# Attention and gated FFN on one core: v products and copies of the first steps rearranged, masks built later

## The chip, the cores and the metric

The kernel runs on one core of one Trainium2 chip. The metric is the device time of one execution in microseconds. Three executions of the kernel before took 215.73, 215.87 and 215.88 us; the median is 215.87.

## What is computed

The input x has 2048 rows of 448 bf16 values. A layer norm without gain gives xn, and the output is x plus two branches that both read xn:

```python
xn = layernorm(x)                                    # per row, eps 1e-5
q, k, v = split(xn @ wqkv)                           # 16 heads of 28 columns
scores = q k^T * 28**-0.5, kept where 0 <= i - j < 256
A = softmax(scores) v @ wo
B = (gelu(xn @ w_gate) * (xn @ w_up)) @ w_down       # inner width 1792
out = x + A + B
```

Each query looks at itself and the 255 keys before it.

## The kernel before

The rows are taken as 16 tiles of 128, in four blocks (`qb`) of 512 rows. The 448 columns of xn are held transposed in `xnT` as three chunks of 128 and one of 64; the last chunk stands twice, in partitions 0 to 63 and in 64 to 127. So a product over the columns is three matmuls of 128 rows and a "half" of 64 rows. Two halves that use different row groups of TensorE can run side by side. For v, `v_dense(t, pv)` (line 219) issues the three full chunks of row tile t and `v_half` (222) the half, in the upper row group for odd t and the lower for even t; `v_copy` (225) then moves the PSUM bank into `v_sb`. For q and k, the heads stand in four groups `g` of four heads; `proj` issues three full chunks, `qk_halves` the half of q (lower row group) and of k (upper), and `qk_copies` (242) moves q through ScalarE, or another engine if one is passed, and k through VectorE.

Nothing is scheduled by a planner: the program runs in a manual schedule, and each engine executes its instructions in the order in which the Python code emits them. For block 0 the order is written as a list `plan` with one entry for each of nine steps of attention. A step `i` emits, in this order: sometimes the product of probabilities with v for a finished head group (`pv`, tile `ov`); its score matmuls (tile `sc`, line 599) into the only score buffer; one exp on ScalarE over 128 x 2048 (line 603) into `p_sb`; the causal and window masking on GpSimd (POOL) by two or three `affine_select` instructions (line 527); and then whatever `plan[i]` lists. An entry `(u, 3)` advances the generator `u` three times. In block 0, `u` first runs `gen_qk` (259) for the groups 1, 2 and 3, three advances per group (q chunks; k chunks; halves and copies), and then `gen_up` (408), seven advances for each up projection `p` of the FFN (tile `ue`, seven pairs of 64-row matmuls, then two copies into `hT`, line 418). Other entries are functions: `stat(t)` takes the row statistics of tile t on VectorE, `rstd` turns them into a scale on ScalarE, `norm(t)` writes the normalised rows on VectorE (line 169), and `dma_transp(t)` transposes them into `xnT` through a DMA of the SP queue (line 175). The functions `ahead`, `ahead2` and `ahead3` (706 to 737) hold such work for the tiles 4 to 7, the exchanges of half columns (`swap`, SP queue), `fill_pads` on POOL (lines 283 and 285) and the weight loads that follow on the SP queue.

PSUM for all of this comes from four banks, `b0` to `b3`. A list `spare` holds the free ones:

```python
    def take(name, cols=QB, tag=None):
        tag = tag or spare[0]
        spare.remove(tag)
    def give(*tiles):
        for ps in tiles:
            spare.append(held.pop(id(ps))[0])
```

A bank is given back in the program as soon as its copy has been emitted; on the chip the next user waits until the copy is done. So the order in which tiles are given decides which copy a later product waits for. Before the first step the v tiles 0 and 1 have been copied, and the tiles `pvs[2]` (bank b2) and `pvs[3]` (b3) are open: `v_dense(3)` is issued ahead of step 0 (line 702), `v_dense(2)` in step 1. Their halves and copies are passed to `gen_qk` as `others`: tile 3 with group 1, tile 2 with group 2.

The weights of q and k are copied from the loaded `wraw` into padded layouts `wqp` and `wkp` by `pads` (646; the copies are line 651), group by group: group 0 early, group 1 on VectorE, and groups 2 and 3 together on VectorE (line 704). `masks` are 0/1 patterns for the blocks from 1 on. VectorE fills them with ones (line 133), and `make_masks` (109) cuts them with 18 `affine_select` instructions on POOL (line 115), ahead of step 0. They are first used in block 1 (line 517).

After the attention steps of a block, `gated` (422) runs seven gate projections (`gt`, line 401), and after each multiplies into `hT`; it calls `hook(2 * p)` (780) after projection p, which emits softmax sums and scalings and the norms of tiles 8 to 11.

Of the kernel before, what the change touches and what calls it, by code (L numbers as in the profile page):

```python
# [17 lines left out]
P = 128  # L18
# [8 lines left out]
def kernel(  # L27
# [11 lines left out]
    nc = tc.nc  # L39
# [133 lines left out]
    def dma_transp(t):  # L173

        nc.sync.dma_start_transpose(out=xnT[:, :, t * P:(t + 1) * P], in_=xns.pop(t)[:, :, :].rearrange("p a b -> p (a b)"))
# [12 lines left out]
    def mm3(ps, lhs, rhs, start, stop):  # L188
        for c in range(3):
            nc.tensor.matmul(ps, lhsT=lhs(c), rhs=rhs(c), start=start and c == 0, stop=stop and c == 2,  # L190
                             skip_group_check=True)
# [24 lines left out]
            spare.append(held.pop(id(ps))[0])  # L216


    def v_dense(t, pv):
        mm3(pv, lambda c: xnT[:, c, t * P:(t + 1) * P], lambda c: wv[:, c, :], True, False)  # L220

    def v_half(t, pv):
        mm_half(pv, xnT[:, 3, t * P:(t + 1) * P], wv[:, 3, :], t % 2, False, True)

    def v_copy(t, pv, copy):
        copy(out=v_sb[:, t, :, 0:Dh], in_=pv.rearrange("p (h d) -> p h d", d=Dh))
        give(pv)
# [14 lines left out]
    def qk_copies(qb, g, pq, pk, q_copy=nc.scalar.copy):  # L242
        q_copy(out=qT[:, g, ring(qb)], in_=pq)
        nc.vector.tensor_copy(out=kT[:, g, qb * QB:(qb + 1) * QB], in_=pk)
        if not (qb == 0 and g == 0):
            give(pq, pk)
        done.add((qb, g))
# [11 lines left out]
    def gen_qk(gs, others):  # L259

        for g in gs:
            pq = take("pq")
            proj(pq, wqp, 0, g)
            yield 650
            pk = take("pk")
            proj(pk, wkp, 0, g)
            yield 650
            if g in others:
                v_half(*others[g])
            qk_halves(0, g, pq, pk)  # L270
            if g in others:
                v_copy(*others[g], nc.vector.tensor_copy)
            qk_copies(0, g, pq, pk)
            yield 360

    def fill_pads(last):
# [408 lines left out]
    proj(pq, wqp, 0, 0)  # L685
    proj(pk, wkp, 0, 0)
    nc.vector.tensor_copy(out=w3p[:, :, 0:Dh], in_=wraw[:, 3, 0:D].rearrange("p (h d) -> p h d", d=Dh))
    nc.vector.memset(masks[:, 0, 0, 0:1], 1.0)
    make_masks()
    stat(4)  # L690
    rstd(4, 1)
    stat(5)
# [8 lines left out]
    pvs.append(take("pv", D, "b3"))  # L701
    v_dense(3, pvs[3])
    for dst in (wqp, wkp):
        pads(nc.vector.tensor_copy, dst, slice(2, 4))

    def ahead():
        norm(4)
# [2 lines left out]
        for hi in range(2):  # L710
            nc.sync.dma_start(out=wvs[64 * hi:64 * hi + 64, :, :], in_=wv64[1 - hi])

    def ahead2():
        stat(6)
        stat(7)
        rstd(5, 3)

    def ahead3():
        for t in (5, 6, 7):
            norm(t)  # L720
            dma_transp(t)
        swap(1, 4, 2)
        swap(1, 6, 2)
        fill_pads(False)
        swap_weights()
        load_ffn(wg, B_w_gate, slice(0, 3))
        nc.sync.dma_start(out=x_sb[:, 12:16, :], in_=xv[:, 12:16, :])
        load_ffn(wu, B_w_up, slice(5, 7))
        load_ffn(wg, B_w_gate, slice(3, 7))
        wo_v = A_wo.rearrange("(g j d) n -> j d g n", g=4, j=4)  # L730
        for j in range(4):
            nc.sync.dma_start(out=wo[32 * j:32 * j + Dh, :, :], in_=wo_v[j])
        for k in range(0, NF, 4):
            n = min(4, NF - k)
            nc.sync.dma_start(out=wd[:, k:k + n, :], in_=rows(B_w_down, k, n))

    for qb in range(NB):
        if qb in (1, 3):
            tc.mark_branch_hint_location("general", hint="LikelyTaken",
                                         engines=[mybir.EngineType.DVE if qb == 1 else mybir.EngineType.PE])  # L740
        early = ()
        if qb == 0:
            new_hT(0)
            early = (0, 1, 2, 3, 4)
            u = chain(gen_qk((1, 2, 3), {1: (3, pvs[3]), 2: (2, pvs[2])}), gen_up(0, (1, 2, 3, 0, 4), (3, 4)))
            w = gen_pairs(1, (("v", 0), ("v", 2), ("k", 0), ("k", 1), ("k", 2)))
            plan = [[(u, 2), ahead, (u, 1)], [lambda: v_dense(2, pvs[2]), (u, 2), ahead2, (u, 1)],
                    [lambda: spare.append(spare.pop(1)), (u, 2), ahead3, (u, 4)], [lambda: stat(8), (u, 11)],
                    [lambda: stat(9), (u, 7), lambda: stat(10), (u, 7), lambda: fill_pads(True)], ["sums", (u, 7)],
                    ["inverse", "scale", (w, 11)], [(w, 10)],  # L750
                    [lambda: stat(11), (w, 7), lambda: rstd(8, 4), "sums", "inverse", (w, 7)]]
        else:
            d = gen_down(qb - 1)
            if qb < 3:
                u = gen_pairs(qb + 1, (("v", 0), ("k", 0), ("v", 2), ("k", 1), ("k", 2)))
                plan = [[(d, 14)], [(d, 11)], [(d, 11)], [(u, 7)], [(d, 18)], ["sums", (u, 7), "inverse"], [(u, 12)],
                        [(u, 9)], [lambda: q_last(qb + 1, nc.vector.tensor_copy), (d, 6), "sums", "inverse"], [(d, 12)]]
                if qb == 1:
                    for i in range(4):
                        plan[i].insert(0, lambda t=12 + i: stat(t))  # L760
                    plan[4].append(lambda: rstd(12, 4))
                    plan[1] = plan[1][:1] + [lambda: q_last(1, nc.vector.tensor_copy), (d, 8)]
                    plan[2] = plan[2][:1] + [(d, 14), lambda: collect(1)]
                    plan[4].append(lambda: deliver(1))
            else:
                new_hT(3)
                early = (1, 2, 3, 4, 5, 6)
                u = gen_up(3, early)
                plan = [[(d, 14)], [(d, 4), (u, 5)], [(u, 9)], [(u, 7)], [(d, 18)], [(u, 7)], [(d, 13)], [(d, 5), (u, 4)],
                        [(u, 10)], [(d, 18)]]  # L770
        if qb in (1, 2):
            swap(qb + 1)
        score_pool(1)
        rest, after, flush = attention(qb, plan)
        nc.scalar.preload_act_table(ACT.Gelu_apprx_tanh)
        score_pool(2)
        if qb not in hTs:
            new_hT(qb)

        def hook(f):  # L780
            after(f)
            if qb in (1, 2) and f == 4:
                collect(qb + 1)
            if qb in (1, 2) and f == 10:
                deliver(qb + 1)
            t = ({0: 8, 4: 9, 8: 10, 10: 11} if qb == 0 else {4: 12, 6: 13, 8: 14, 10: 15} if qb == 1 else {}).get(f)
            if t is not None:
                norm(t)
                dma_transp(t)

        gated(qb, early, rest, flush, hook)
        if qb < NB - 1:
            nc.scalar.preload_act_table_set("natural_log_exp_and_others")
# [151 lines left out]
```

## Time and profile before

| | us |
|---|---|
| median of three runs | 215.87 |
| profiled execution | 215.72 |
| its span on the core | 214.0 |

| engine | busy us | share of the span | instructions |
|---|---|---|---|
| TensorE (PE) | 208.4 | 97% | 2722 |
| VectorE (DVE) | 161.9 | 76% | 357 |
| ScalarE (ACT) | 130.3 | 61% | 121 |
| GpSimd (POOL) | 46.7 | 22% | 78 |

The granted TensorE clock is full throughout. Block 0's steps begin at 11.7 us with the first scores, and its gates at 37.4 us. In a timeline row stand the start in us, the length in us, engine, source line, operation, what is written from what, shapes, how many instructions are merged, and in brackets the idle time before them with the work that ended it. PE rows of merged matmuls overlap at their ends, since matmuls are pipelined. In a group row stand the count, then busy time and mean length in ns, then idle time before. In a tile's or a line's rows the lengths are least, median and greatest in ns.

### The profile page before, as it was taken

The page shows a single profiled execution, that of the slowest core. Times are in us where ns is not written, and L with a number is a line of the kernel's source. Part 1 is how long each engine was busy: PE and PEld are TensorE (multiplying, and loading weights), DVE is VectorE, ACT ScalarE, POOL GpSimd, SP SyncE. Part 2 cuts the span into 40 slices and gives each one's busy share as a digit, 9 for nine tenths or more (in the row PEclk, how much of TensorE's full clock was granted, in tenths as well). Part 3 has the DMA queues.
Part 4 walks back from the last instruction along what each step waited for, and adds up shares of the span by engine and source line. Part 5 has one row for each costly group of instructions (what it writes and reads, how often), then busy time and mean ns, then how long its engine had stood idle before and what let it go on. Part 6 is the DMA issues. An engine that isn't in the chain of part 4 may idle for free.

```text
span 214.0 us, 6358 instructions
## 1 busy us (share of the span) xinstructions
PE 208.4 (97%) x2722; PEld 100.8 (47%) x2722; DVE 161.9 (76%) x357; ACT 130.3 (61%) x121; POOL 46.7 (22%) x78
## 2 busy tenths in 40 slices
PE   7999999999999999999999999999999999999993
PEld 2433444444454545444445445444444444544892
DVE  7899998999866995698546998495449699569621
ACT  4699578566677986423777896532678577456000
POOL 5287658423000211022000202022000021106001
PEclk9999999999999999999999999999999999999999
DMA  6999669994411101002230000200000000000011
GB/s 190 273 214 224 100 168 255 228 319 60 100 50 30 38 0 41 8 19 56 49 95 25 25 0 27 44 0 3 0 26 0 25 3 25 21 3 2 23 35 39
DMA packets 23297, 15.21 MB, mean 71 GB/s; under 512 B 8960, under 2 KB 23136, under 8 KB 23264
## 3 DMA queue, kind: packets, MB, share of 16 engines
q1 hardware_dynamic: 22320, 14.47, 30.2%
q8 instruction: 22, 0.36, 0.7%
q10 hardware_dynamic: 944, 0.29, 0.6%
q14 instruction: 11, 0.09, 0.2%
HBM read 9.03 MB, written 2.18 MB: 52 GB/s over the span
## 4 chain that ended last, share of the span: by engine, by line
PE 94%; DVE 1%; ACT 1%; DMA 1%; issue 1%; DVEq 0%; ACTq 0%
PE po L359 26%; PE gt L401 20%; PE u L401 12%; PE ue L401 8%; PE sc L599 7%; PE pq L333 7%; PE ov L569 5%; PE pv L319 4%; PE pq L190 2%; PE pv L190 1%; DMA x_sb<-in_A_x_dram 1%; ACT p_sb L603 1%; DVE st L154 1%; PE s L190 1%; PE pk L190 1%
## 5 line engine op out<-in xcount | busy, mean ns | idle before, releaser
L603 ACT ACTIVATE p_sb<-sc 128x2048 bf16<-128x2048 f32 x39 | 73.3, 1878 | 21.1 <-PE sc L599 13.5
L536 POOL TENSOR_TENSOR oN<-oc,l 128x512 bf16<-128x512 f32 x16 | 22.5, 1406 | 138.0 <-DVE l L549 138.0
L441 ACT ACTIVATE p_sb<-gt 128x1024 bf16<-128x1024 f32 x28 | 28.7, 1024 | 33.7 <-PE gt L401 32.9
L359 PE MATMUL po<-wd,hT 128*128 128x448 bf16 (+1 forms) x266 | 47.9, 323 | 0.0
L401 PE MATMUL gt<-xnT,wg 64*128 64x512 bf16 x224 | 45.6, 376 | 0.0
L401 PE MATMUL gt<-xsw,wg 64*128 64x512 bf16 x168 | 40.7, 376 | 0.0
L517 DVE TENSOR_TENSOR p_sb<-p_sb,masks 128x256 bf16<-128x256 bf16 (+1 forms) x90 | 30.1, 389 | 4.5 <-ACT p_sb L603 4.5
L449 DVE TENSOR_TENSOR hT<-p_sb,u 128x512 bf16<-128x512 bf16 x34 | 22.0, 681 | 15.0 <-PE u L401 15.0
L359 PEld LDWEIGHTS <-hT 128*128 128x128 bf16 x266 | 24.6, 98 | 16.2 <-issue 1.2
L401 PEld LDWEIGHTS <-wg 64*128 64x128 bf16 x392 | 18.6, 94 | 23.0 <-issue 1.3
L401 PEld LDWEIGHTS <-wu 64*128 64x128 bf16 x392 | 18.4, 94 | 23.1 <-issue 2.2
L401 PE MATMUL u<-xnT,wu 64*128 64x512 bf16 x136 | 28.1, 376 | 0.0
L401 PE MATMUL u<-xsw,wu 64*128 64x512 bf16 x102 | 24.7, 376 | 0.0
L367 DVE TENSOR_TENSOR res<-po,x_sb 128x448 bf16<-128x448 f32 (+1 forms) x17 | 10.1, 592 | 17.4 <-PE po L359 17.4
L401 PE MATMUL ue<-xnT,wu 64*128 64x512 bf16 x88 | 18.3, 377 | 0.0
L401 PE MATMUL ue<-xsw,wu 64*128 64x512 bf16 x66 | 16.5, 377 | 0.0
L599 PE MATMUL sc<-qT,kT 28*64 28x320 bf16 (+7 forms) x648 | 16.4, 261 | 0.1
L527 POOL TENSOR_SCALAR_AFFINE_SELECT p_sb<-p_sb 128x512 bf16<-128x512 bf16 (+1 forms) x21 | 14.2, 701 | 6.6 <-ACT p_sb L603 6.5
L359 PE MATMUL po<-wo,oN 128*128 128x448 bf16 (+1 forms) x76 | 15.1, 323 | 0.0
L599 PEld LDWEIGHTS <-kT 28*64 28x64 bf16 (+1 forms) x648 | 7.7, 102 | 13.5 <-issue 12.2
L418 DVE CAST hT<-ue 128x512 bf16<-128x512 f32 x20 | 12.7, 676 | 0.6 <-PE ue L401 0.4
L554 DVE TENSOR_TENSOR oc<-oc,ov 128x512 f32<-128x512 f32 x12 | 8.2, 686 | 4.8 <-ACT oc L553 4.7
(102 smaller groups left out, 271.5 us busy)
## 6 DMA issues: line engine op xcount, KB each, us to landing
out_dram<-res SPq DMA_DIRECT2D x15, 112.0 KB
x_sb<-in_A_x_dram SPq DMA_DIRECT2D x3, 448.0 KB
wd<-in_B_w_down_dram SPq DMA_DIRECT2D x3, 448.0 KB
xsw<-xnT SPq DMA_DIRECT2D x6, 192.0 KB
wu<-in_B_w_up_dram SPq DMA_DIRECT2D x2, 560.0 KB
wg<-in_B_w_gate_dram SPq DMA_DIRECT2D x2, 448.0 KB
wg<-in_B_w_gate_dram SPq DMA_DIRECT2D x2, 336.0 KB
wraw<-in_A_wqkv_dram SPq DMA_DIRECT2D x2, 252.0 KB
```

The source lines that it names most:

```text
L190: nc.tensor.matmul(ps, lhsT=lhs(c), rhs=rhs(c), start=start and c == 0, stop=stop and c == 2, skip_group_check=True)
L333: nc.tensor.matmul(ps, lhsT=w.rearrange("p h d -> p (h d)"), rhs=xchunk(qb, hi, c, qb * QB, QB), start=c == 0, stop=c == 6, tile_position= ...
L359: nc.tensor.matmul(po[:, a:b], lhsT=x[:, k, cs], rhs=wt[:, k, lo + a:lo + b], start=(n == a == 0), stop=(n == len(terms) - 1), skip_group_ ...
L401: nc.tensor.matmul(ps, lhsT=w[64 * hi:64 * hi + 64, c, p * P:(p + 1) * P], rhs=xchunk(qb, hi, c, qb * QB, QB), start=c == 0, stop=c == 6, ...
L418: copy(out=hTs[qb][:, p + 7 * i, :], in_=us[i])
L441: nc.scalar.activation(out=ges[p][:, :, :], in_=gt[:, :, :], func=ACT.Gelu_apprx_tanh)
L449: nc.vector.tensor_tensor(out=hT[:, p + 7 * i, :], in0=ge[:, i, :], in1=u, op=ALU.mult)
L517: nc.vector.tensor_tensor(out=reg, in0=reg, in1=m, op=ALU.mult)
L527: nc.gpsimd.affine_select(out=reg, in_=reg, pattern=mid + [[1 if diag else -1, min(w, P)]], compare_op=ALU.is_ge, fill=0.0, base=0 if diag ...
L536: nc.gpsimd.tensor_tensor(out=oN[:, g, :], in0=oc[:, :], in1=inv, op=ALU.mult)
L599: nc.tensor.matmul(ss[k0:k0 + nk, j, col:col + nq], lhsT=kT[r, g, kt * P + k0:kt * P + k0 + nk], rhs=qT[r, g, ring(qb).start + q0:ring(qb) ...
L603: nc.scalar.activation(out=p_sb[:, :, 0:ncol], in_=ss[:, :, 0:ncol], func=ACT.Exp, scale=SCALE)
```

## The change

- `v_dense` gets a parameter `cs` that says which chunks it issues. Tile 2's chunks 0 and 1 are now issued in step 0, between group 1's k chunks and group 1's halves, and chunk 2 at the head of step 1.
- `gen_qk` takes a list of v tiles for a group. The halves of tiles 2 and 3 are both issued with group 2, one after the other, and so are their copies; group 1 has none.
- Group 2's q copy goes from ScalarE to VectorE.
- The pads of groups 2 and 3 go from VectorE to POOL.
- `make_masks` moves from the place ahead of step 0 to `hook(6)` of block 0, behind gate projection 3, and the one-element memset that preceded it is dropped.
- `stat(6)` moves from `ahead2` to the end of `ahead`. In step 2, `norm(5)` and its transpose come ahead of group 3's halves and copies, and `norm(6)`, `norm(7)` and all that follows them come behind. The rotation of `spare` at the head of step 2 is dropped.
- Step 2 issues two chunk pairs of the first up projection instead of three, step 3 one more.

```diff
-    def v_dense(t, pv):
-        mm3(pv, lambda c: xnT[:, c, t * P:(t + 1) * P], lambda c: wv[:, c, :], True, False)
+    def v_dense(t, pv, cs=range(3)):
+        for c in cs:
+            nc.tensor.matmul(pv, lhsT=xnT[:, c, t * P:(t + 1) * P], rhs=wv[:, c, :], start=c == 0, stop=False, skip_group_check=True)
...
-            if g in others:
-                v_half(*others[g])
+            for t, pv in others.get(g, ()):
+                v_half(t, pv)
             qk_halves(0, g, pq, pk)
-            if g in others:
-                v_copy(*others[g], nc.vector.tensor_copy)
-            qk_copies(0, g, pq, pk)
+            for t, pv in others.get(g, ()):
+                v_copy(t, pv, nc.vector.tensor_copy)
+            qk_copies(0, g, pq, pk, nc.vector.tensor_copy if g == 2 else nc.scalar.copy)
             yield 360
...
-    nc.vector.memset(masks[:, 0, 0, 0:1], 1.0)
-    make_masks()
     stat(4)
...
     for dst in (wqp, wkp):
-        pads(nc.vector.tensor_copy, dst, slice(2, 4))
+        pads(nc.gpsimd.tensor_copy, dst, slice(2, 4))
...
+        stat(6)
+
     def ahead2():
-        stat(6)
         stat(7)
         rstd(5, 3)
 
     def ahead3():
-        for t in (5, 6, 7):
+        norm(5)
+        dma_transp(5)
+
+    def ahead4():
+        for t in (6, 7):
             norm(t)
             dma_transp(t)
         swap(1, 4, 2)
...
-            u = chain(gen_qk((1, 2, 3), {1: (3, pvs[3]), 2: (2, pvs[2])}), gen_up(0, (1, 2, 3, 0, 4), (3, 4)))
+            u = chain(gen_qk((1, 2, 3), {2: ((2, pvs[2]), (3, pvs[3]))}), gen_up(0, (1, 2, 3, 0, 4), (3, 4)))
...
-            plan = [[(u, 2), ahead, (u, 1)], [lambda: v_dense(2, pvs[2]), (u, 2), ahead2, (u, 1)],
-                    [lambda: spare.append(spare.pop(1)), (u, 2), ahead3, (u, 4)], [lambda: stat(8), (u, 11)],
+            plan = [[(u, 2), ahead, lambda: v_dense(2, pvs[2], range(2)), (u, 1)],
+                    [lambda: v_dense(2, pvs[2], range(2, 3)), (u, 2), ahead2, (u, 1)],
+                    [(u, 2), ahead3, (u, 1), ahead4, (u, 2)], [lambda: stat(8), (u, 12)],
...
             after(f)
+            if qb == 0 and f == 6:
+                make_masks()
```

## The prediction

> **What bounds the kernel now.** I read the page's head and the chain of waits first, then the table of stretches over the first steps, then each engine's timeline there.
>
> ```profile
> span 214.0 us, 6358 instructions
> PE 94%; DVE 1%; ACT 1%; DMA 1%; issue 1%; DVEq 0%; ACTq 0%
> 11.60:14.10 2.50, 2.38 (x19) 0.82 (x19) 2.30 (x9) 2.23 (x3) 2.07 (x10) 1.00 1.11 217
> 19.60:23.00 3.40, 3.40 (x52) 1.50 (x50) 3.37 (x7) 2.13 (x2) 3.40 (x12) 1.00 1.34 132
> ```
>
> The columns of a stretch are its length and the busy time of PE, PEld, DVE, ACT and POOL. The chain is TensorE almost throughout, so only what makes TensorE idle, or gives it less work, counts. But from 19.6 to 23.0 VectorE is as full as TensorE (3.37 of 3.40; its rows below show no idle time from 16.80 on), while in step zero (11.6 to 14.1) it has 0.2 us free. Work that goes from the early stretch into the later one lands on an engine with no room.
>
> ```profile
> 12.65 0.81 PE L190 MATMUL pk<-xnT,wkp 128*128 128x512 bf16 x3
> 13.40 0.36 PE L196 MATMUL pv<-wv,xnT 64*128 64x448 bf16 x1
> 13.40 0.39 PE L196 MATMUL pq<-xnT,w3p 64*128 64x512 bf16 x1
> 13.60 0.38 PE L196 MATMUL pk<-xnT,w3p 64*128 64x512 bf16 x1
> 14.10 0.40 PE L599 MATMUL sc<-qT,kT 28*128 28x384 bf16 x8
> 14.43 0.74 PE L190 MATMUL pv<-wv,xnT 128*128 128x448 bf16 x3
> 15.01 0.81 PE L190 MATMUL pq<-xnT,wqp 128*128 128x512 bf16 x3
> 16.40 0.36 PE L196 MATMUL pv<-wv,xnT 64*128 64x448 bf16 x1
> 16.91 0.40 PE L599 MATMUL sc<-qT,kT 28*128 28x128 bf16 x8
> 22.41 0.68 PE L569 MATMUL ov<-p_sb,v_sb 128*32 128x128 bf16 x20
> 23.35 0.39 PE L401 MATMUL ue<-xnT,wu 64*128 64x512 bf16 x1
> 12.17 1.88 ACT L603 ACTIVATE p_sb<-sc 128x2048 bf16<-128x2048 f32 x1 [0.27 <-PE sc L599]
> 13.94 0.58 ACT L243 CAST qT<-pq 128x512 bf16<-128x512 f32 x1
> ```
>
> Step one's scores begin at 14.10, because the single score buffer comes free when step zero's exp ends (12.17 + 1.88 = 14.05). From the last half before a score to the score takes 0.31 us where nothing waits (the second half starts 0.20 after the one at 16.40, the scores at 16.91), so 13.60 to 14.10 holds 0.19 us of stall. A pair of 64-row halves that use different row groups starts together (13.40 and 13.40); one that doesn't takes a slot of its own, 0.20 us (13.60). These two are all that TensorE can win here: 0.39 us.
>
> **The change, part by part.**
>
> *TensorE.* Two v chunks (3 chunks take 14.43 to 15.01, so 0.19 us each) move ahead of group 1's halves: 12.65, three matmuls of 0.216 ((0.81 - 0.38) / 2), two chunks, and 0.10 of turnaround (13.30 to 13.40 before) put the halves at 13.78, now one pair instead of two slots, and step one's scores stay at 14.10. The stall is filled. Then one chunk, to 14.63. But group 2's q projection now takes another PSUM bank. Before, v of tile 3 was copied first and gave its bank to the head of the list. Now nothing is given before group 1's q and k, so group 2's q gets the bank that group 1's q has just left, and waits for its ACT copy: halves end at 13.78 + 0.39 = 14.17, copy 0.58, plus two handovers of 0.05 (as from 14.05 to 14.10): 14.84. Bounds: 0 (were the bank another) to 0.21. It starts at 14.84 against 15.01, and the halves of v at 16.23 against 16.40. Of 0.39, 0.17 is left. ACT's next exp starts about 0.14 later behind that copy; scores of step two (16.74) don't wait for it.
>
> *VectorE from the first v copy to the first up copy.* This decides. Rows:
>
> ```profile
> 12.23 0.27 DVE L651 COPY wkp<-wraw 128x336 bf16<-128x336 bf16 x1
> 12.42 0.37 DVE L651 COPY wqp<-wraw 128x672 bf16<-128x672 bf16 x1
> 16.80 0.62 DVE L226 CAST v_sb<-pv 128x448 bf16<-128x448 f32 x1 [0.30 <-PE pk L196]
> 17.34 0.68 DVE L244 CAST kT<-pk 128x512 bf16<-128x512 f32 x1
> 17.93 2.18 DVE L169 TENSOR_SCALAR xn<-x_sb,mv_all,rstd_all 128x448 bf16<-128x448 bf16 x6
> 18.36 0.80 DVE L169 TENSOR_SCALAR xn<-x_sb,mv_all,rstd_all 128x64 bf16<-128x64 bf16 x3
> 18.87 1.25 DVE L169 TENSOR_SCALAR xn<-x_sb,mv_all,rstd_all 128x64 bf16<-128x64 bf16 x3
> 20.02 0.68 DVE L244 CAST kT<-pk 128x512 bf16<-128x512 f32 x1
> 20.63 0.61 DVE L154 BATCH_NORM_STATS2 st<-x_sb 128x6 f32<-128x448 bf16 x1
> 21.37 2.45 DVE L418 CAST hT<-ue 128x512 bf16<-128x512 f32 x4
> L169 DVE TENSOR_SCALAR xn<-x_sb,mv_all,rstd_all x6: 286/383/732, 17.9 to 19.4; 128x448 bf16<-128x448 bf16 x3, 128x64 bf16<-128x64 bf16 x3
> 19.44 1.23 POOL L527 TENSOR_SCALAR_AFFINE_SELECT p_sb<-p_sb 128x512 bf16<-128x512 bf16 x2 [1.14 <-ACT p_sb L603]
> 20.62 0.20 POOL L283 COPY wqp<-wraw 128x16 bf16<-128x16 bf16 x1
> L817 POOL CAST g<-res 128x224 f32<-128x224 bf16 x1 | 0.4, 370 | 13.3 <-DVE res L367 13.3
> L102 POOL MEMSET v_sb<- 128x768 bf16 x1 | 1.5, 1523 | 0.0
> ```
>
> Before, 16.80 to 21.37 is 4.57 us: v 0.54 start to start, k 0.60, three norms at 0.51 (18.36 to 18.87, the second parts of two), k 0.60, statistics 0.74, which is 4.02, and 0.55 in which norms stood. One of them shows why: a norm of 64 columns takes 286 ns, one took 732, starting at 19.38 while Pool's select ran 19.44 to 20.08. After, the stretch holds v of tile 3 as well (+0.54; it was at 13.79, in the free time) and group 2's q (+0.60; it was on ACT): 5.16. Statistics 6 leaves, but from ahead of 16.80, where VectorE had 0.30 idle anyway, so it gains nothing.
>
> The margin that TensorE has on this queue: the third up projection (23.35) uses banks that the second and third of the four up copies free. The third ends at 21.37 + 2 x 0.59 + 0.66, about 23.22, with 0.06 of handover 23.28. So 0.08 us. Beyond it TensorE waits one for one. With the v copy 0.17 earlier and no waits for Pool the first up copy starts at 16.63 + 5.16 = 21.79, 0.42 late, of which 0.34 reaches TensorE. The smaller waits on the way (v copies for group 3's q bank, some 0.2; group 2's k for an up bank, some 0.1) fall within this and aren't added.
>
> *Waits for Pool.* Norm 5 now runs at about 18.9 to 19.4, and step two's two selects start at about 19.1 (its exp runs some 0.3 earlier, with no q copy ahead): 0 to 1.2 us, I take the row's 732 - 286 = 0.44. Norms 6 and 7 come after group 3's k, at 20.4 to 21.4, on top of Pool's nine pad copies (from 20.62 before, 0.15 apart, about 1.4 us); before they were done at 20.11. No row shows a Pool copy beside such an operation: 0 to 1.4, I take the nearest, one blocked operation by a select, 0.44.
>
> *The big pads on Pool.* 0.37 each leave VectorE where it had room: no gain. Length on Pool: 0.20 + (672 - 16) x (0.37 - 0.20) / (224 - 16) = 0.74 us by the copies; up to 1.3 by the strided memset (1.98 ns an element). Group 2 needs them at 14.84, covered. But k's pad can only start when its weights land, and VectorE's own small k pad (12.23) waits for the same transfer:
>
> ```profile
> 9.35 0.63 DVE L154 BATCH_NORM_STATS2 st<-x_sb 128x6 f32<-128x448 bf16 x1 [0.15 <-DMA x_sb<-in_A_x_dram]
> wraw<-in_A_wqkv_dram SPq DMA_DIRECT2D x2, 252.0 KB
> 9.30:11.40 2.10, 2.10 (x13) 0.70 (x11) 1.98 (x5) 1.02 (x4) 1.81 (x9) 1.00 1.04 243
> ```
>
> x lands at 9.35; two pieces of 252 KB behind it at 243 GB/s need 2.1 us: 11.5, later if the up weights share. Pool then copies to 12.3 or beyond, and the 12.23 copy stands; group 1's k projection (12.65, 0.15 after that copy) goes with it, and all of step one. 0 to 0.8; I take 0.25.
>
> *Masks.*
>
> ```profile
> 9.28 5.04 POOL L115 TENSOR_SCALAR_AFFINE_SELECT masks<-masks 64x64 bf16<-64x64 bf16 x18 [5.62 <-DVE masks L688]
> 48.82 1.62 POOL L536 TENSOR_TENSOR oN<-oc,l 128x512 bf16<-128x512 f32 x1 [3.20 <-DVE l L549]
> 55.16 0.83 DVE L517 TENSOR_TENSOR p_sb<-p_sb,masks 128x256 bf16<-128x256 bf16 x3 [0.63 <-ACT p_sb L603]
> ```
>
> They queue behind 48.82 + 1.62 = 50.44 and end at 55.5; the first use at 55.16 needs the first six (52.1). Between 0 and 0.4 for VectorE, whose result goes to products much later: 0 taken. Behind them Pool has nothing due.
>
> *Queues.*
>
> ```profile
> 18.67 5.04 SPq L175 DMA_TRANSPOSE xnT<-xn  x3
> 29.36 0.36 PE L319 MATMUL pv<-wv,xnT 64*128 64x448 bf16 x1
> ```
>
> SP's transposes 5 to 7, the eight swaps and weight loads behind them follow the norms, about 1 us later for the first and under 1 for the last (it was issued only at 22.5, behind the others); first use is 5.6 us after 23.7, so 0, bounded by 0.3.
>
> **Sum:** 0.34 + 0.25 + 0.44 + 0.44 = 1.47 us. The profiled execution took 215.72 (span 214.0, 1.72 around it), 0.15 under the median shown. 215.72 + 1.47 = 217.2.
>
> The Trainium skill (page "SBUF — State Buffer", section "Who interferes with whom") says that GpSimd and VectorE's two-port modes share one port pair, that whichever starts first holds it for the whole instruction, and that copies and tensor_scalar count among these modes. The trace agrees for selects (732 ns against 286); no row shows a Pool copy. By that rule all blocked terms stand, 217.2; if selects alone held the port, 215.72 + 0.34 + 0.44 = 216.5.
>
> **Rivals.**
> - *Queue without blocking:* the norms slip between Pool's instructions, the k weights land early. 0.34 alone: 216.1, within 0.2% (0.43 us, about what a measurement here tells from no change). For it: some norms took the usual 383 ns beside selects. Against: 0.55 lost in the same place before.
> - *The queue never reaches TensorE:* up copies have more margin than 0.08, or VectorE makes up 0.42. Then the 0.17 won stays: 215.55; with the bank wait gone as well 215.33. It decides if the first up copy starts by 21.45. This is the other side; it barely passes 0.2%.
> - *Long Pool copies:* 1.3 us by the memset's row. The small k pad then stands about 0.8 and the pad copies hold both norms longer: +0.6 and +0.5, 218.3.
>
> **How the numbers follow.** Forecast 0.60; long copies 0.14; queue without blocking 0.16; not reaching TensorE 0.10. Slower 0.74, within 0.2% 0.20, faster 0.06 (part of the last). The range reaches from 215.7, leaving out most of the last, to 218.5, past the long copies; the forecast's own is 216.5 to 217.9.
>
> **What would show it.** Right: step one's scores still at about 14.1 to 14.4, group 2's q projection idle behind the ACT copy, VectorE without idle from about 16.8, its first up copy at 22.2 to 23.5, and the products of step four and the third up projection waiting for VectorE; norms longer than 400 ns beside Pool. Wrong: that up copy before 21.5, Pool copies that don't lengthen VectorE's, or another bank for group 2's q.

## The result and the profile after

The changed kernel took 216.86 us (median of 8 executions, 216.30 to 217.08) against 215.72 (215.49 to 215.88): a ratio of 1.0047 with a 95% interval of 1.0035 to 1.0059, 1.14 us slower. The profiled execution took 216.5 us, 0.8 above that of before (215.72).

The head of the page, the chain of waits, and the table of stretches (length, then busy PE, PEld, DVE, ACT, POOL, then granted clock, mean DMA engines' share and GB/s) of the kernel after:

```profile
span 214.8 us, 6355 instructions
PE 92%; DVE 4%; DMA 1%; issue 1%; ACT 0%; DVEq 0%
11.60:14.10 2.50, 2.45 (x20) 0.92 (x21) 2.12 (x8) 2.17 (x2) 0.00 (x0) 1.00 1.12 220
...
16.70:19.50 2.80, 2.63 (x22) 0.91 (x20) 2.80 (x6) 2.52 (x4) 2.13 (x4) 1.00 1.19 247
19.50:22.80 3.30, 3.13 (x34) 1.21 (x32) 3.27 (x10) 2.07 (x2) 3.30 (x12) 1.00 0.54 94
```

VectorE's share of the chain went from 1% to 4%. In the first stretch TensorE gained (2.45 busy of 2.50, against 2.38), and from 16.7 on VectorE is full (2.80 of 2.80, 3.27 of 3.30) while TensorE stands for 0.34 us in the last two.

TensorE's timeline after (columns as in the prediction):

```profile
11.66 0.40 PE L600 MATMUL sc<-qT,kT 28*128 28x128 bf16 x8
14.09 0.40 PE L600 MATMUL sc<-qT,kT 28*128 28x384 bf16 x8
...
14.83 0.81 PE L190 MATMUL pq<-xnT,wqp 128*128 128x512 bf16 x3
16.22 0.36 PE L196 MATMUL pv<-wv,xnT 64*128 64x448 bf16 x2
16.73 0.40 PE L600 MATMUL sc<-qT,kT 28*128 28x128 bf16 x8
17.30 0.81 PE L190 MATMUL pq<-xnT,wqp 128*128 128x512 bf16 x3 [0.17 <-DVE v_sb L227]
...
18.91 0.38 PE L402 MATMUL ue<-xnT,wu 64*128 64x512 bf16 x1
19.02 0.48 PE L402 MATMUL ue<-xsw,wu 64*128 64x512 bf16 x2
...
22.84 0.68 PE L570 MATMUL ov<-p_sb,v_sb 128*32 128x128 bf16 x20 [0.21 <-DVE hT L419]
23.78 0.39 PE L402 MATMUL ue<-xnT,wu 64*128 64x512 bf16 x1
24.03 0.39 PE L402 MATMUL ue<-xsw,wu 64*128 64x512 bf16 x2
...
27.14 0.40 PE L600 MATMUL sc<-qT,kT 28*128 28x128 bf16 x8
...
210.51 0.55 PE L360 MATMUL po<-wd,hT 128*128 128x224 bf16 x4
```

The rows of before that are needed beside it:

```profile
11.67 0.40 PE L599 MATMUL sc<-qT,kT 28*128 28x128 bf16 x8
...
26.48 0.40 PE L599 MATMUL sc<-qT,kT 28*128 28x128 bf16 x8
...
209.84 0.55 PE L359 MATMUL po<-wd,hT 128*128 128x224 bf16 x4
```

Count from the first scores (11.66 after, 11.67 before). After the change TensorE is 0.17 ahead at the scores of step two (16.73, 16.91). It then gives back 0.24 waiting for a v copy (a projection of group 3 follows its scores by 0.57, not 0.33), 0.11 waiting for a bank of the first up projection (19.02 behind 18.91), about 0.27 in front of the products of step four (22.84) and 0.25 in the third up projection, whose second bank is free at 24.03. That is 0.87, or 0.70 with the lead taken off, and at the scores of step five it is 27.14 - 11.66 - (26.48 - 11.67) = 0.67 behind, at the last products 0.68. So the whole of the traced loss arises between 16.7 and 24.1 us. The 0.1 that is left to the span's 0.8 lies behind the last product.

VectorE's timeline after, and the group row of its norms (least, median and greatest in ns):

```profile
12.23 0.27 DVE L652 COPY wkp<-wraw 128x336 bf16<-128x336 bf16 x1
16.61 1.16 DVE L227 CAST v_sb<-pv 128x448 bf16<-128x448 f32 x2 [0.94 <-PE pv L196]
17.69 0.68 DVE L244 CAST qT<-pq 128x512 bf16<-128x512 f32 x1
...
18.88 0.92 DVE L169 TENSOR_SCALAR xn<-x_sb,mv_all,rstd_all 128x448 bf16<-128x448 bf16 x2
19.71 0.68 DVE L245 CAST kT<-pk 128x512 bf16<-128x512 f32 x1
20.31 1.15 DVE L169 TENSOR_SCALAR xn<-x_sb,mv_all,rstd_all 128x448 bf16<-128x448 bf16 x4
21.38 0.61 DVE L154 BATCH_NORM_STATS2 st<-x_sb 128x6 f32<-128x448 bf16 x1
22.13 2.45 DVE L419 CAST hT<-ue 128x512 bf16<-128x512 f32 x4
L169 DVE TENSOR_SCALAR xn<-x_sb,mv_all,rstd_all x6: 292/384/612, 18.9 to 21.1; 128x448 bf16<-128x448 bf16 x3, 128x64 bf16<-128x64 bf16 x3
```

From the first v copy to the first up copy VectorE has no idle time: 22.13 - 16.61 = 5.52 us, against 4.57 before. The up copies start 0.76 later, and the third ends at 22.13 + 2 x 0.59 + 0.66 = 23.97, which with 0.06 is the 24.03 above.

Pool's timeline after (the nine pad copies are represented by two of them):

```profile
9.54 0.74 POOL L652 COPY wqp<-wraw 128x672 bf16<-128x672 bf16 x1 [5.89 <-DMA wraw<-in_A_wqkv_dram]
10.55 0.75 POOL L652 COPY wkp<-wraw 128x672 bf16<-128x672 bf16 x1 [0.26 <-DMA wraw<-in_A_wqkv_dram]
...
19.12 1.23 POOL L528 TENSOR_SCALAR_AFFINE_SELECT p_sb<-p_sb 128x512 bf16<-128x512 bf16 x2 [0.67 <-ACT p_sb L604]
20.45 0.33 POOL L286 COPY wqp<-wraw 128x48 bf16<-128x48 bf16 x1
...
21.67 0.22 POOL L286 COPY wqp<-wraw 128x48 bf16<-128x48 bf16 x1
...
51.07 5.22 POOL L115 TENSOR_SCALAR_AFFINE_SELECT masks<-masks 64x64 bf16<-64x64 bf16 x18
```

The large pads ran at 9.54 and 10.55, so the k weights had landed by 10.55, about a microsecond before the estimate of 11.5; the small k pad on VectorE (12.23) came at the same time as before. The masks end at 56.29; TensorE is 0.67 behind before them, at step five, and 0.68 at its last products, so they cost it nothing here.

### The profile page after: what moved, and what is told of

The parts are those of the page before. It is cut to its first block, busy times and chain, and to the rows that moved or that the text cites. A ratio compares the mean times of both kernels' runs of the same rounds, so it can differ in the third digit from the quotient of the medians.

```text
span 214.8 us, 6355 instructions
## 1 busy us (share of the span) xinstructions
PE 208.4 (97%) x2718; PEld 101.0 (47%) x2722; DVE 161.5 (75%) x355; ACT 129.9 (60%) x120; POOL 48.5 (23%) x80
## 4 chain that ended last, share of the span: by engine, by line
PE 92%; DVE 4%; DMA 1%; issue 1%; ACT 0%; DVEq 0%
PE po L360 26%; PE gt L402 20%; PE u L402 12%; PE ue L402 7%; PE pq L334 6%; PE sc L600 6%; PE ov L570 5%; PE pv L320 4%; PE pq L190 2%; PE pv L221 1%; DMA x_sb<-in_A_x_dram 1%; DVE st L154 1%; DVE xn L169 1%; PE s L190 1%; PE pk L190 1%
## 5 line engine op out<-in xcount | busy, mean ns | idle before, releaser
L402 PE MATMUL ue<-xsw,wu 64*128 64x512 bf16 x66 | 15.9, 377 | 0.0
```

Of the source, the lines that this page charges most:

```text
L402: nc.tensor.matmul(ps, lhsT=w[64 * hi:64 * hi + 64, c, p * P:(p + 1) * P], rhs=xchunk(qb, hi, c, qb * QB, QB), start=c == 0, stop=c == 6, ...
```

## The experiments

Theory A is the prediction's: VectorE's queue, lengthened by two copies and by norms that stand behind Pool, makes TensorE wait. The main rivals were that Pool's large pads or the masks made the loss, that one copy alone did, and that the queue alone did it without any Pool part. The variants start from the changed kernel, the one-chunk kernel from the one before. The last column comes from each kernel's one traced execution: the scores of step five less the first scores, against 26.48 - 11.67 = 14.81 before, in us; plus is later.

| kernel | median (range) us | ratio to before, 95% | step five |
|---|---|---|---|
| control: changed kernel again | 216.36 (216.05–216.66) | 1.0026 [1.0011, 1.0041] | +0.74 |
| large pads on VectorE | 216.45 (216.34–216.66) | 1.0032 [1.0020, 1.0044] | +0.75 |
| group 2's q on ScalarE | 216.28 (216.01–216.50) | 1.0022 [1.0014, 1.0031] | +0.71 |
| up copies on ScalarE | 216.20 (216.05–216.75) | 1.0020 [1.0010, 1.0030] | +0.43 |
| v halves and copies first | 216.24 (215.99–216.91) | 1.0020 [1.0004, 1.0037] | +0.47 |
| masks early | 216.58 (216.48–216.99) | 1.0039 [1.0024, 1.0053] | +1.12 |
| pads held behind the small one | 216.38 (216.12–217.34) | 1.0036 [1.0023, 1.0050] | +0.74 |
| pads held across the small one | 216.50 (216.05–216.90) | 1.0028 [1.0013, 1.0043] | +0.83 |
| statistics later | 216.27 (215.70–217.06) | 1.0022 [1.0003, 1.0040] | +0.16 |
| one chunk alone, on the kernel before | 215.84 (215.50–216.64) | 1.0006 [0.9992, 1.0020] | +0.08 |
| reworked | 215.62 (215.35–216.11) | 0.9995 [0.9984, 1.0006] | -0.16 |
| reworked, statistics later | 215.61 (215.32–215.82) | 0.9993 [0.9984, 1.0003] | -0.16 |

The kernels ran on three chips, each beside the kernel before, which had medians of 215.71 to 215.80; so compare the ratios. Executions of one kernel differ by half a microsecond and more here. By their ratios the variants with one part undone (large pads, group 2's q, up copies, v halves, statistics) can't be told from the control: their intervals overlap. What they show is in the last column, TensorE's order in one traced execution of each.

**The large pads on VectorE again.**

```diff
-        pads(nc.gpsimd.tensor_copy, dst, slice(2, 4))
+        pads(nc.vector.tensor_copy, dst, slice(2, 4))
```

> The changed kernel with one part undone: the pads of groups 2 and 3 are on VectorE again. Theory A (VectorE's queue from the first v copy to the first up copy is the loss, 0.66 us in the profiled run; the further 0.3 to 0.5 us of the slower among the changed kernel's executions, 216.85 to 217.08 against 216.30 to 216.50, is the small k pad standing behind Pool's k pad when its weights land late): VectorE had 0.9 us idle ahead of the first v copy, so the pads cost nothing there, the queue stays, and the median falls to 216.2 to 216.5 with a spread under 0.3. Rival B (the Pool pads have nothing to do with the slower executions): median stays at 216.8 to 216.9 and the spread at 0.8. Rival C (the pads on VectorE delay tile 4 and the statistics enough to lengthen the queue): above 217.

The median is where it was expected, but so is the control's (216.36) with the pads on Pool. Nothing was gained: +0.75 at step five against +0.67 and +0.74 with them on Pool. In these traced executions the pads on Pool cost nothing, and cannot be the cause.

**Group 2's q copy back on ScalarE.**

```diff
-            qk_copies(0, g, pq, pk, nc.vector.tensor_copy if g == 2 else nc.scalar.copy)
+            qk_copies(0, g, pq, pk)
```

> The changed kernel with one part undone: group 2's q copy is on ScalarE again. Theory A (queue): VectorE's first up copy comes 0.60 us earlier, about 21.5 instead of 22.13, the third up projection about 0.5 earlier (0.1 to 0.2 behind the kernel before), the median 0.45 to 0.6 below the changed kernel's 216.86, so 216.25 to 216.4. Rival D (TensorE loses by its own waits ahead of it: group 3's q bank 0.24, the up bank 0.11): the queue has nothing to do with it, and the median stays within 0.15 of 216.86.

The median is at the level expected, but the control's is too, and the mechanism expected was missed in the trace: the first up copy came 22.31 - 11.81 = 10.50 behind the first scores, no earlier than in the changed kernel (22.13 - 11.66 = 10.47), and TensorE was +0.71 behind. Two other delays took the place of the copy. The first is of a kind that the prediction had priced: the k weights landed late. Timelines of this kernel:

```profile
11.40 0.75 POOL L652 COPY wkp<-wraw 128x672 bf16<-128x672 bf16 x1 [0.80 <-DMA wraw<-in_A_wqkv_dram]
11.67 0.61 DVE L652 COPY wqp<-wraw 128x336 bf16<-128x336 bf16 x1
14.49 0.40 PE L600 MATMUL sc<-qT,kT 28*128 28x384 bf16 x8
```

Pool's copy held VectorE's small pad, which took 0.61 us where such a copy takes 0.27, and step one's scores came 14.49 - 11.81 = 2.68 behind the first, not 2.43: 0.25 lost. That is the amount of the prediction's 0.25, in one execution, though here the pad held was the small q pad and not the small k pad. The two traces of the changed kernel don't have it. The second is that norms 6 and 7 ran beside Pool's select and took 1.42 (20.14 to 21.56) against 1.07. So this trace doesn't show what the q copy alone is worth.

**Masks early.**

```diff
+    nc.vector.memset(masks[:, 0, 0, 0:1], 1.0)
+    make_masks()
...
-            if qb == 0 and f == 6:
-                make_masks()
```

> The changed kernel with one part undone: the masks are made ahead of step zero again. That puts Pool's two pads behind 18 selects (5 us from about 9.3), so they run from about 14.3 on and group 2 waits for its weights. Theory A: masks in the gates cost nothing, but the early masks with Pool pads behind them do: q's pad ends at about 15.1 and k's at 15.9, group 2's q projection starts at 15.1 instead of 14.8 and its k at 15.9, and the median is 0.3 to 0.7 above the control. Rival E (masks in the gates are part of the loss): at or below the control's median.

Timelines of this kernel:

```profile
14.36 0.74 POOL L652 COPY wqp<-wraw 128x672 bf16<-128x672 bf16 x1
15.16 0.82 PE L190 MATMUL pq<-xnT,wqp 128*128 128x512 bf16 x3 [0.38 <-POOL wqp L652]
```

The pads follow the masks at 14.36 instead of 9.54, and group 2's q projection waits 0.38 us for the first. TensorE is 0.38 further behind than in the control, the median 0.22. So moving the masks into the gates makes the room that the pads need on Pool, and the rival that this move is part of the loss has nothing for it.

**Up copies on ScalarE**: it takes the second copy of the first two up projections too. The projections come in the order 1, 2, 3, 0, 4, so the entries 3 and 4 of before are the third and the fifth.

```diff
-gen_up(0, (1, 2, 3, 0, 4), (3, 4))
+gen_up(0, (1, 2, 3, 0, 4), (1, 2, 3, 4))
```

> The changed kernel with ScalarE taking one copy of each of the first two up projections too (it took one of the fourth and of the fifth before), where ScalarE stood idle from 21.9 to 23.9. Nothing ahead of the first up copy is altered. Theory A: the third up projection waits for banks that are now free 0.6 to 1.2 earlier, the products of step four start when TensorE reaches them (about 22.6 instead of 22.84), and the median falls by 0.5 to 0.65 to 216.2 to 216.35. Rival D (TensorE's own waits ahead) or a cause behind the first steps (masks): no change within 0.15.

```profile
23.00 0.68 PE L570 MATMUL ov<-p_sb,v_sb 128*32 128x128 bf16 x20 [0.21 <-DVE hT L419]
23.94 0.60 PE L402 MATMUL ue<-xsw,wu 64*128 64x512 bf16 x2
```

The products of step four came at 23.00 - 11.82 = 11.18 behind the first scores, as in the changed kernel (22.84 - 11.66): the expected time for them was missed, because the very first up copy stayed on VectorE and they wait for that one. What disappeared is the 0.25 in the third up projection: its second stream starts beside its first (23.94, 23.93), and step five is at +0.43 instead of +0.67. So both waits are for VectorE's up copies, one after the other. The median (216.20) came to the level expected, but only 0.16 below the control's, which ran on another chip.

**v halves and copies ahead of group 2's q.**

```diff
-            u = chain(gen_qk((1, 2, 3), {2: ((2, pvs[2]), (3, pvs[3]))}), ...
+            u = chain(gen_qk((1, 2, 3), {}), ...
...
-                    [lambda: v_dense(2, pvs[2], range(2, 3)), (u, 2), ahead2, (u, 1)],
+                    [lambda: v_dense(2, pvs[2], range(2, 3)), v_halves, (u, 2), ahead2, (u, 1)],
```

(`v_halves` issues both halves, then both copies.)

> The changed kernel with the halves and copies of v tiles 2 and 3 moved ahead of group 2's q chunks, into the time in which group 2's q waits for its bank (14.62 to 14.83) and VectorE is idle (15.67 to 16.61). Theory A: the two v copies (1.08 us) leave the full part of VectorE's queue, group 3's q finds its bank free, step two's scores come at about 16.7 as in the changed kernel, the first up copy at 20.9 to 21.4, and TensorE is no longer held: 0.1 to 0.2 us below the kernel before (215.5 to 215.7), 1.2 below the changed kernel. Rival B (the slower executions have another cause that stays): 216.0 or more. Rival D's waits vanish here as well, so this run alone does not tell A from D; it tells what the pairing of the halves is worth when nothing waits.

Missed by half a microsecond. The waits for the v copy are gone, but the statistics of tile 7 now stand behind the v copies on VectorE, ScalarE's scale waits for them, and a norm was held by Pool's select:

```profile
17.38 0.30 ACT L159 ACTIVATE lnv<-mv_all,eps_t 128x3 f32<-128x3 f32 x1 [0.49 <-DVE mv_all L155]
19.86 1.69 DVE L169 TENSOR_SCALAR xn<-x_sb,mv_all,rstd_all 128x448 bf16<-128x448 bf16 x4
44.45 0.39 PE L402 MATMUL gt<-xsw,wg 64*128 64x512 bf16 x2 [0.16 <-DMA wg<-in_B_w_gate_dram]
```

The pair of norms takes 1.61 (19.86 to 21.47) against 1.07 in the changed kernel. The queue is hardly shorter, in another order: the first up copy comes 22.21 - 11.95 = 10.26 behind the first scores, against 10.47. The last row is a wait of another kind: the gate weights came late, and by the last products, which start at 211.14, TensorE was 211.14 - 11.95 - (209.84 - 11.67) = 1.02 behind, half a microsecond more than at step five.

**The control**, the changed kernel unchanged beside the next two kernels and the masks:

> The changed kernel as it is, for the median and the spread on the chip of the three runs beside it. Its executions fell into two groups before, 216.30 to 216.50 and 216.85 to 217.08. Theory A (the upper group are executions in which the k weights land late and one of VectorE's small pads stands behind a Pool pad; seen in the profile of the run with q on ScalarE: 606 ns instead of 267, scores of step one 0.25 late): both groups again. Median 216.3 to 217.0.

The expected upper group didn't come: the twelve executions lie between 216.05 and 216.66. The loss in the median was 0.56 us here against 1.14 in the first comparison, with TensorE behind by 0.74 and 0.67 in their traces. What lies outside TensorE's work differs between executions: from the last product to the end of the span it was 214.8 - 210.51 = 4.29 in the first and 3.94 in the control.

**Pads held behind, and across, VectorE's small k pad.** A tiny copy on Pool makes the large pads wait for the last small pad, or for group 0's k copy, so that in the second kernel they meet the small pad. One kernel has the first of these two copies, the other the second:

```diff
+    hold = work.tile([P, 8], bf16, name="hold")
+    nc.gpsimd.tensor_copy(out=hold[:, 0:4], in_=wkp[:, 2, 7, 0:4])   # behind
+    nc.gpsimd.tensor_copy(out=hold[:, 0:4], in_=kT[:, 0, 0:4])       # across
```

> The changed kernel with Pool's two pads held behind VectorE's last small pad (one tiny Pool copy of 4 columns reads what that pad wrote), so that they start at about 12.7, end at about 14.3, and can't stand in front of the small pads however late the weights land. Theory A: the upper group of executions goes, median 216.3 to 216.5, spread 0.3; group 2's weights (needed at 14.8 and 15.5) still come in time. Rival F (the upper group comes from elsewhere: the gate weights' landing, or the norms' collisions): the spread stays at 0.7 and the median as the control's.

> The changed kernel with Pool's two pads held behind the first k copy (11.6), so that they run from about 11.8 to 13.3 in every execution, across VectorE's small k pad (12.23). Theory A: the small k pad takes 0.4 to 1.2 us instead of 0.27, group 1's k projection starts 0.25 to 0.9 late, step one's scores likewise, and the median is 217.0 or more, 0.3 to 0.8 above the run with the pads behind. Rival G (the port is not what blocks, only the late landing itself): as the run with the pads behind.

Held behind, neither the median nor the spread became smaller (216.12 to 217.34), which speaks against the pads as the source of the spread, though the six executions with the pads on VectorE spread by 0.32 only. Held across, the pads ran at 11.97 and 12.66:

```profile
11.97 0.74 POOL L652 COPY wqp<-wraw 128x672 bf16<-128x672 bf16 x1
12.40 0.44 DVE L652 COPY wkp<-wraw 128x336 bf16<-128x336 bf16 x1
12.66 0.74 POOL L652 COPY wkp<-wraw 128x672 bf16<-128x672 bf16 x1
```

The small pad took 0.44 instead of 0.27, and TensorE was 0.09 further behind than in the control, well below what was expected. The pad met the first Pool copy when 11.97 + 0.74 - 12.40 = 0.31 of it was left, lost 0.17, and was done with the second not in front of it: VectorE gets in between two Pool copies. The norm behind it then met the second one and took 0.97 instead of 0.59, in time that VectorE had to spare.

**Statistics of tile 8 four steps later**, and nothing else:

```diff
-                    [(u, 2), ahead3, (u, 1), ahead4, (u, 2)], [lambda: stat(8), (u, 12)],
+                    [(u, 2), ahead3, (u, 1), ahead4, (u, 2)], [(u, 12)],
...
-                    ["inverse", "scale", (w, 11)], [(w, 10)],
+                    ["inverse", "scale", (w, 11)], [lambda: stat(8), (w, 10)],
```

> The changed kernel with the statistics of tile 8 (0.74 us on VectorE, not needed before step eight) moved from ahead of the first up copy to step seven. Nothing else is touched. Theory A (VectorE's queue up to the first up copy is what holds TensorE): counted from the first scores, the first up copy comes 0.74 earlier (9.7 instead of 10.46), TensorE meets the products of step four and the third up projection without waiting, and stands 0.14 to 0.2 behind the kernel before instead of 0.67 to 0.75, what its two own waits cost (group 3's q bank, the up bank). Median 0.5 below the changed kernel on its chip, so some 216.0. Rival D (the waits ahead of the queue are the loss): 0.6 or more behind, as the changed kernel.

This takes 0.7 us out of VectorE's queue and leaves every product, bank and Pool instruction in its place:

```profile
11.72 0.40 PE L600 MATMUL sc<-qT,kT 28*128 28x128 bf16 x8
21.44 2.58 DVE L419 CAST hT<-ue 128x512 bf16<-128x512 f32 x4
26.69 0.40 PE L600 MATMUL sc<-qT,kT 28*128 28x128 bf16 x8
```

and from its waits (total us, times, longest):

```profile
PEld L402 <- DMA wg<-in_B_w_gate_dram: 0.4, 1, 0.4
```

The first up copy comes 9.72 behind the first scores instead of 10.47. The waits for up copies are gone, and of 0.67 only 0.16 stays, about the v copy's and the bank's 0.35 less the lead of 0.17. For TensorE's order this run settles it: the up copies' place in VectorE's queue made half a microsecond of its loss. For the time it doesn't. The median is 0.3 above the 216.0 expected and 0.56 above the kernel before, as the control's was. In its trace a weight load of the gates waits for `wg` again, and by the last products TensorE is 210.34 - 11.72 - (209.84 - 11.67) = 0.45 behind: 0.29 of what was won is lost there. So a second limit, the landing of the gate weights, stands close behind the first; whether it decides the timed executions, of this kernel or of the changed one, isn't shown.

**One chunk of tile 2's v in step zero, alone**, on the kernel before:

```diff
-            plan = [[(u, 2), ahead, (u, 1)], [lambda: v_dense(2, pvs[2]), (u, 2), ahead2, (u, 1)],
+            plan = [[(u, 2), ahead, lambda: v_dense(2, pvs[2], range(1)), (u, 1)],
+                    [lambda: v_dense(2, pvs[2], range(1, 3)), (u, 2), ahead2, (u, 1)],
```

> The kernel before with one part of the change alone: one chunk (not two) of tile 2's v in step zero, ahead of group 1's halves. Banks, copies and VectorE's order stay. Theory A: 0.19 of the 0.19 us stall ahead of step one's scores is filled and nothing else moves; TensorE is 0.15 to 0.19 ahead of the kernel before from step two on, VectorE follows 0.15 to 0.19 earlier. Median 0.1 to 0.2 below the kernel before, 215.5 to 215.7. If VectorE's queue has no room even for that, the lead is gone at the third up projection (its margin before was 0.08).

Missed, and instructive: TensorE was 0.18 ahead at the scores of step two (16.78 - 11.72) and had lost that at those of step three (19.74). Two delays lie between. Group 1's halves come later behind the extra chunk, with them VectorE's copy of v tile 3 (14.04, 13.79 before) and the statistics behind it; the scale waits for these, and ScalarE's next q copy (17.21) is late. It ends at 17.78, and group 3's k, in the bank that it frees, starts at 17.83, some 0.07 late. Then the second stream of the first up projection starts 0.20 behind its first (19.00 and 18.80; together before, 18.87 and 18.86). What it waited for the profile doesn't show.

```profile
16.77 0.30 ACT L159 ACTIVATE lnv<-mv_all,eps_t 128x3 f32<-128x3 f32 x1 [0.29 <-DVE mv_all L155]
17.83 0.81 PE L190 MATMUL pk<-xnT,wkp 128*128 128x512 bf16 x3
19.00 0.39 PE L402 MATMUL ue<-xsw,wu 64*128 64x512 bf16 x2
```

**Reworked**: the filled step zero stays; v halves and copies go ahead of group 2's q, with the statistics of tile 7 ahead of the copies; group 2's q on ScalarE, the large pads on VectorE, and the three norms together as before.

```diff
-            qk_copies(0, g, pq, pk, nc.vector.tensor_copy if g == 2 else nc.scalar.copy)
+            qk_copies(0, g, pq, pk)
...
-    def ahead2():
+    def v_halves():
+        for t in (2, 3):
+            v_half(t, pvs[t])
         stat(7)
-        rstd(5, 3)
+        for t in (2, 3):
+            v_copy(t, pvs[t], nc.vector.tensor_copy)
...
-                    [lambda: v_dense(2, pvs[2], range(2, 3)), (u, 2), ahead2, (u, 1)],
-                    [(u, 2), ahead3, (u, 1), ahead4, (u, 2)], [lambda: stat(8), (u, 12)],
+                    [lambda: v_dense(2, pvs[2], range(2, 3)), v_halves, (u, 2), lambda: rstd(5, 3), (u, 1)],
+                    [(u, 2), ahead3, ahead4, (u, 4)], [lambda: stat(8), (u, 11)],
```

> The changed kernel with: halves and copies of v tiles 2 and 3 ahead of group 2's q chunks and behind the statistics of tile 7, group 2's q copy on ScalarE, the large pads on VectorE, and norms 5 to 7 ahead of group 3 as in the kernel before. Theory A: VectorE's stretch from group 2's k copy to the first up copy holds one k copy, three norms, one k copy and one statistic, less than before; both banks of v are free when group 3 starts; TensorE keeps what the filled stall gives: 0.15 to 0.2 ahead of the kernel before at step two's scores and still at the third up projection. Median 215.4 to 215.7, at most just told from the kernel before. If TensorE has lost it again by the third up projection, something else than VectorE's queue and the banks holds it.

> The reworked kernel with the statistics of tile 8 in step seven as well. Theory A: TensorE isn't held by VectorE in the reworked kernel, so the same as that one to 0.05 at the third up projection (0.15 to 0.2 ahead of the kernel before). If the reworked one is still held, this one is earlier by what holds it.

TensorE's timeline of the reworked kernel:

```profile
11.73 0.40 PE L600 MATMUL sc<-qT,kT 28*128 28x128 bf16 x8
16.80 0.40 PE L600 MATMUL sc<-qT,kT 28*128 28x128 bf16 x8
26.38 0.40 PE L600 MATMUL sc<-qT,kT 28*128 28x128 bf16 x8
```

TensorE keeps its 0.16 from step two to the end, as expected, and with less in VectorE's queue (the second kernel) it keeps no more. So once the up copies are in time, what is left of the filled stall is all there is. In the time this is 0.1 us with an interval that holds no change at all: the rework repairs the change, and doesn't measurably beat the kernel before. It undoes several parts at once, so it shows that the timed loss goes with VectorE's order and what follows from it, not how much of it each part made.

## Why the prediction was right, and where its sum was not

The time (217.2 forecast, 216.86 measured, range 215.7 to 218.5) and the direction held. The mechanism is the one predicted: VectorE's up copies come late and TensorE waits for them. But two terms of the sum hardly occurred in the traces, and that the time came so near is partly luck.

- *TensorE.* Right to two hundredths: scores of step one 14.09 (14.10 predicted), group 2's q projection 14.83 (14.84; it follows group 1's q copy, 14.19 + 0.58 = 14.77 and a handover), v halves 16.22 (16.23), scores of step two 16.73 (16.74), first v copy 16.61 (16.63).
- *VectorE's queue, 0.34.* Right. Its length without waits was put at 5.16; with 0.36 of waits it measured 5.52. Up copies 0.76 late (0.77 counted from the first scores), less the margin of 0.08, is 0.69; TensorE lost 0.67. The margin and the one-for-one law behind it held, and the later statistics and the ScalarE up copies showed from the other side that these waits are what the loss is made of. That the smaller waits (0.24 for the v copy, 0.11 for a bank) fall within it held too, since the later waits end at a time that VectorE sets; with the later ones taken away they come to light, 0.16 net.
- *Norm 5 behind Pool's select, 0.44.* Right in kind, somewhat smaller: a norm part took 612 ns against 292 at best, and the pair 0.83 (18.88 to 19.71) against 0.51: 0.32.
- *Norms 6 and 7 beside Pool's pad copies, 0.44.* This step failed. Two norms took 1.07 (20.31 to 21.38) against 1.02: 0.05, and 0.11 in the control. The ones that became longer were Pool's copies, 0.33 against 0.22. A select as the nearest row was the wrong model for a row of short copies: between two of them VectorE gets in.
- *Small k pad behind Pool's, 0.25.* This step failed in the traces of the changed kernel: the small pad kept its 12.23 and 0.27. What failed is the landing time of the weights. Where they did land late, step one lost 0.25 in one trace (group 2's q on ScalarE, by the small q pad) and 0.04 in another (v halves first, whose small k pad took 0.39).
- *Large pads, masks.* Right: 0.74 and 0.75 us each, 0.74 predicted; masks ending at 56.29 hold nobody.
- *The SP queue at 0.* Right for the transposes. The gate weights, issued behind them, were late in the traces of two variants and cost TensorE 0.29 and 0.55 there (statistics later; v halves first), nearly twice the bound of 0.3 at most; whether they are ever late in the timed runs of the changed kernel is open.

The sum by what was measured is 0.34 + 0.32 + 0.05 = 0.71, which is the 0.67 to 0.74 in the traces, and not 1.47. That TensorE figure is nearer to the rival "queue without blocking" (0.34) than to the forecast, and the control's 0.56 is too: of that rival's conditions the early k weights and the norms slipping between Pool's copies came, and only norm 5 was held; the 1.14 of the first comparison is nearer to the forecast, but no trace shows where its part above the 0.8 of the traced execution arises. Of the spread between executions only parts were found (the end of the span 3.94 to 4.29, weights landing at different times), not the cause. Of the prediction's own signs, the ones for it came, with the up copy at 22.13 just ahead of its 22.2 to 23.5, and one against it came in part: Pool's short copies hardly lengthened VectorE's norms. The rival that the queue never reaches TensorE fell: the up copies started at 22.13, past the 21.45 from which it decides. The one of long Pool copies fell with 0.74.

## What to carry to other kernels

A stall that is filled on the busiest engine is worth only what the engine that empties its banks can follow: sum that engine's instructions from the first moved one to the first one that frees a bank, and compare with the margin there before counting the gain. Where work moves to another engine's queue, price it by the instructions that already stand there in that stretch, and look at what moves behind it: here two of the variants brought a new wait because statistics came later behind a copy. A block by another engine should be priced by what is left of the one instruction that is met, not by the sum of a run of short ones. And a wait that is taken away can uncover the next: half a microsecond less in TensorE's order didn't show in the median of the statistics run.

## What the runs showed of the hardware

- Pool copies do hold VectorE's bf16 copies: 0.61 us instead of 0.27 beside a 0.75 us Pool copy. That agrees with the Trainium skill (page "SBUF — State Buffer", section "Who interferes with whom"), which the prediction could support for selects alone. In four traces a small pad began with 0.48, 0.31, 0.26 and 0.21 us of a large Pool pad still to run, and lost 0.34, 0.17, 0.12 and 0.07: 0.14 less than the rest each time. In a fifth, with 0.07 left, it lost nothing.
- Who is held depends on who comes first, as that section says: in those four traces Pool's copy had begun first. Beside a row of short Pool copies VectorE lost 0.05 and 0.11 in two norms in the changed kernel's two traces, and in the first of them three Pool copies took 0.05 to 0.14 longer. In the prediction's row (732 ns from 19.38, the select from 19.44) the two starts are too close to tell who came first.
- The k weights behind Pool's second large pad landed at very different times in different executions: the pad began at 10.55, 11.04, 11.40 and 12.03 us in four of them, with the first scores at 11.66 to 11.95.
- When only one of two side-by-side streams of 64-row products waits (24.03 behind 23.78), the whole projection ends later by that wait: it took 27.14 - 24.03 = 3.11 us from the later start, and 26.48 - 23.35 = 3.13 before, where both start together.
